# A second kv buffer for a long convolution that runs beside attention, with its load cut into four parts

## The chip, the cores and the metric

The kernel runs on one core of a Trainium2 chip. Its time is the device time of one execution in microseconds (us). The engines are called TensorE or PE, VectorE (DVE), ScalarE (ACT), GpSimd (POOL) and SyncE (SP), which here only issues DMAs.

## What is computed

Two independent computations share one kernel, and their results stand side by side in the output. A is a gated convolution over S = 2048 positions and D = 640 channels: a convolution of 4 taps over k, a product with v, a convolution of length 2048 for each channel, and a product with q. B is plain attention with 32 heads of 20 channels.

```python
def A(q, k, v, shift_k, ssm_k, ssm_D):            # [1, 2048, 640]
    k_pad = pad(k, ks - 1 rows in front)           # ks = 4
    k_shift = sum(k_pad[:, t:t+S] * shift_k[:, ks-1-t] for t in range(ks))
    kv = k_shift * v
    y  = causal_convolution(kv, ssm_k)             # 2048 taps for each channel, by FFT in the reference
    return q * (y + kv * ssm_D)

def B(x, wqkv, wo):                                # H = 32, Dh = 20
    q, k, v = split(x @ wqkv)
    p = softmax(q @ k.T * Dh ** -0.5)
    return (p @ v) @ wo

out = concatenate([A, B], axis=-1)                 # [1, 2048, 1280]
```

## The kernel before

**Attention.** The 32 heads form 8 groups of four; the 2048 queries form 4 blocks of 512, the keys 16 blocks of 128. A tile of scores is 128 keys by 512 queries of one head, and there are 8 x 4 x 16 x 4 = 2048 of them. PE makes the scores (`S_task`, L629), two or three tiles to neighbouring banks of PSUM. ScalarE takes the exponentials of these two or three in one instruction (L671) and writes them to one of 44 slots in SBUF. Some tiles go to VectorE instead: L691 scales a tile out of PSUM, and lines L726 to L731 with L721 or L723 finish the exponential for two tiles together with a polynomial. `want_vec` opens such a chain only when VectorE has little work waiting. PE multiplies the exponentials with v (L749).

**Convolution.** First the short convolution (`C_task`, PE L559, VectorE L580) makes kv, which is written to a scratch tensor in DRAM, `kvr_scratch`. The long convolution is then 40 tasks of 16 channels each (`conv_task`), in 8 blocks of five. Its matmuls (L1022, 128 in a task) take their weights from `HK`, four buffers that are filled from `kext_scratch` (`hk_load`, 16 DMAs in a task), and their moving data from `KVX`, two small buffers in turn. `KVX` for one task is copied by GpSimd out of the kv tile `KVr` in two instructions (`kvx_build`, L994). The kv tile of a block has 80 channels, and so serves five tasks. It is one buffer of 64 x 80 elements in each partition, loaded by `kvr_load` as four DMAs for four sets of 32 partitions, of 320, 240, 160 and 80 KB; what the parts leave open is cleared once by four GpSimd memsets (L972). The call that builds `KVX` for a block's fifth task also asks for the load of the next block, which has to wait until that task's copies have read the tile.

`kvx_build(t + 2)` is called at the end of task t, so a block's last build and the next block's load come at the end of its third task, and the next block's first build comes at the end of its fourth.

**Order.** The whole program is written out by a planner when the kernel is built. It keeps a model clock for each engine, appends to each engine's list whatever is ready by that model, and writes waits for semaphores from its records of who reads and writes which buffer (`Buf`, `Prog.op`). On the chip each engine runs its list in order. PE's loop puts the scores first and fits the rest, convolution included, into the slack that ScalarE leaves. The convolution is paced (`conv_wants`): task n starts when a proportional share of the score tiles has been issued, so that the last starts 230 tiles before the end at the latest. GpSimd's clears and copies wait in a list (`pool_work`), of which one of the first four is placed beside a suitable step of VectorE (`pool_beside`). DMAs on SP are kept in a list too (`P.late`) and appended by `flush` in the order in which the planner finds them ready, with a model of their landing. All DMAs of the trace show the helper's line L239.

**Memory.** The tiles of the short convolution and those of the long one share the region `R`, whose size is the larger of two sums, `ph0` and `ph1`; `conv_setup`, which runs after the last `C_task`, makes the records for the second use.

## Time and profile before

| | |
|---|---|
| three runs | 827.39, 829.12 and 830.6 us; median 829.12 |
| the profiled execution | 825.78 us, its span on the core 824.0 us |
| mean granted TensorE clock | 0.998 |
| convolution matmuls L1022 | 5120, from 168.6 to 766.7 us |
| copies L994 | 80, from 164.6 to 732.2 us, 0.64 us each |
| clears L972 | 4, 0.57 us each, from 144.8 to 149.8 us |
| kext loads | 640 of 136 KB, 3.8 us to landing (median) |
| kvr loads | 32 in 8 groups of four, first group issued at 149.8 us |

In the lines of the profile, "R" stands for everything in the shared region and for the slots of the exponentials, "PS" for PSUM, "issue" for time in which an engine waited for nothing that the profile shows. A group's line has its count, busy time in us and mean in ns of one, then the idle time ahead of it with what ended it. A timeline's line begins with the start and the length in us; instructions of one line that follow each other closely are merged, with the idle time ahead of them in brackets.

### The profile page before, as it was taken

What the parts mean: (1) busy time and instruction counts of PE and PEld (TensorE: products, weight loads), DVE (VectorE), ACT (ScalarE), POOL (GpSimd) and SP (SyncE); (2) the same over time, 40 slices, a digit from 0 to 9 for tenths busy, and PEclk for the clock granted to TensorE, in tenths of its full rate; (3) what the DMA queues carried; (4) which work ended last, traced back from release to release, by engine and by line L of the source; (5) the groups of instructions that cost most, each with busy time, mean ns of one, the idle gap of its engine ahead of it and who ended that gap; (6) DMA issues with size and microseconds to landing.
All of it is one profiled execution on the core that took longest, in us unless ns stands there. A gap on an engine that the chain in (4) does not pass through costs nothing.

```text
span 824.0 us, 27547 instructions
## 1 busy us (share of the span) xinstructions
PE 802.6 (97%) x11750; PEld 368.8 (45%) x11750; DVE 772.6 (94%) x1609; ACT 804.6 (98%) x762; POOL 94.4 (11%) x163
## 2 busy tenths in 40 slices
PE   8999999999999999999999999999999999999997
PEld 4444442244455454444445445544444444453422
DVE  2399999999899999999999999999999999999996
ACT  5999999999899999999999999999999999999996
POOL 3000000111001002210101121000111201010110
PEclk9999999999999999999999999999999999999999
DMA  9934243659878989885898877656887968384111
GB/s 169 313 79 90 44 85 48 137 112 196 171 179 172 197 170 202 180 192 113 167 212 186 171 180 169 151 120 136 181 187 162 192 148 182 98 182 127 28 50 41
DMA packets 163226, 121.94 MB, mean 148 GB/s; under 512 B 72832, under 2 KB 161408, under 8 KB 162848
## 3 DMA queue, kind: packets, MB, share of 16 engines
q1 hardware_dynamic: 160912, 117.06, 66.4%
q0 software_dynamic: 736, 2.75, 0.9%
q8 instruction: 93, 1.52, 0.8%
q10 hardware_dynamic: 1456, 0.37, 0.2%
q14 instruction: 29, 0.24, 0.1%
HBM read 106.83 MB, written 10.61 MB: 143 GB/s over the span
## 4 chain that ended last, share of the span: by engine, by line
ACT 54%; PE 22%; DVE 22%; issue 1%; DMA 1%
ACT R L671 54%; PE PS L629 7%; DVE XV L691 6%; PE PS L1022 6%; PE PS L749 3%; PE PS L484 3%; DVE XF L728 2%; DVE XF L731 2%; DVE XF L726 1%; DVE R L721 1%; DVE XF L727 1%; DVE XF L729 1%; PE PS L846 1%; PE PS L530 1%; DVE R L723 1%; DVE R L1041 1%
## 5 line engine op out<-in xcount | busy, mean ns | idle before, releaser
L671 ACT ACTIVATE R<-PS 128x1024 bf16<-128x1024 f32 (+1 forms) x754 | 800.3, 1265 | 4.4 <-PE PS L629 4.0
L629 PE MATMUL PS<-QT,KT 20*128 20x512 bf16 x2048 | 293.9, 385 | 11.1 <-ACT R L671 5.1
L691 DVE TENSOR_SCALAR XV<-PS 128x512 uint16<-128x512 f32 x291 | 197.7, 684 | 9.1 <-PE PS L629 7.5
L1022 PEld LDWEIGHTS PS<-R 128*128 128x128 bf16 x5120 | 163.3, 97 | 81.3 <-issue 80.8
L1022 PE MATMUL PS<-R 128*128 128x32 bf16 (+5 forms) x5120 | 197.7, 184 | 1.6 <-issue 1.5
L749 PE MATMUL PS<-R,V_sb 128*21 128x512 bf16 x2048 | 160.8, 385 | 0.7 <-DVE R L721 0.2
L629 PEld LDWEIGHTS PS<-QT,KT 20*128 20x128 bf16 x2048 | 73.5, 91 | 195.5 <-ACT R L671 155.0
L731 DVE TENSOR_TENSOR XF<-XF 128x1024 bf16<-128x1024 bf16 (+1 forms) x151 | 100.3, 666 | 0.4
L728 DVE TENSOR_TENSOR XF<-XF 128x1024 bf16<-128x1024 bf16 (+1 forms) x151 | 100.3, 666 | 0.1
L994 POOL COPY R<-R 128x256 uint32<-128x256 uint32 x80 | 51.0, 638 | 392.9 <-DVE XV L691 98.8
L721 DVE TENSOR_TENSOR R<-XF,XV 128x1024 uint16<-128x1024 bf16 x93 | 63.6, 684 | 0.1
L749 PEld LDWEIGHTS PS<-R,V_sb 128*21 128x21 bf16 x2048 | 35.3, 89 | 61.8 <-issue 36.4
L390 PE MATMUL PS<-Zt 128*128 128x512 bf16 x206 | 60.9, 392 | 1.2 <-DVE Zt L384 1.0
L729 DVE TENSOR_SCALAR XF<-XF 128x1024 bf16<-128x1024 uint16 (+1 forms) x151 | 61.6, 410 | 0.1
L727 DVE TENSOR_SCALAR XF<-XF 128x1024 bf16<-128x1024 uint16 (+1 forms) x151 | 61.3, 410 | 0.3
L726 DVE TENSOR_SCALAR XF<-XV 128x1024 uint16<-128x1024 uint16 (+1 forms) x151 | 60.7, 410 | 0.1
L1061 POOL TENSOR_TENSOR R<-R 128x160 bf16<-128x160 bf16 x64 | 31.3, 488 | 182.2 <-DVE XF L726 51.2
L484 PE MATMUL PS<-xT,WQ 128*20 128x512 bf16 (+1 forms) x660 | 48.4, 375 | 1.4 <-DVE XV L691 0.8
L484 PE MATMUL PS<-xT,WKV 128*20 128x512 bf16 (+1 forms) x660 | 48.7, 376 | 0.5 <-DVE XV L691 0.2
L723 DVE TENSOR_TENSOR R<-XF,XV 128x512 uint16<-128x512 bf16 x105 | 40.5, 419 | 0.2
L530 PE MATMUL PS<-WKV,xT 128*128 128x160 bf16 x320 | 35.8, 235 | 0.5
L473 DVE CAST QT<-PS 128x512 bf16<-128x512 f32 (+1 forms) x33 | 22.0, 668 | 9.2 <-PE PS L484 9.0
(58 smaller groups left out, 352.3 us busy)
## 6 DMA issues: line engine op xcount, KB each, us to landing
R<-kext_scratch SPq DMA_DIRECT2D x640, 136.0 KB, 3.8
R<-in_A_v_dram SPq DMA_DIRECT2D x4, 640.0 KB, 5.0
kext_scratch<-in_A_ssm_k_dram POOLq DMA_DIRECT2D x1, 2560.0 KB, 13.4
kvr_scratch<-R SPq DMA_DIRECT2D x128, 20.0 KB
R<-kvr_scratch SPq DMA_DIRECT2D x8, 320.0 KB, 5.1
R<-in_A_q_dram SPq DMA_DIRECT2D x32, 80.0 KB, 3.7
out_dram<-R SPq DMA_DIRECT2D x32, 80.0 KB, 3.3
R<-kvr_scratch SPq DMA_DIRECT2D x8, 240.0 KB, 5.4
```

What stands on the lines that cost most here:

```text
L484: ins = e.matmul(bank[bk][32 * i:32 * i + DH, 0:n], Wt[:, cc, off + i * DH:off + (i + 1) * DH], xT[:, cc, x0:x0 + n], start=(cc == 0), sto ...
L629: ins = e.matmul(bank[b0 + i], KT[32 * u:32 * u + DH, g % 2, kb * 128:(kb + 1) * 128], QT[32 * u:32 * u + DH, qs(qc, g), :], start=True, s ...
L671: P.op("act", lambda e: e.activation(P_sb[:, s0:s0 + m, :], PS[:, b0 * 512:(b0 + m) * 512].rearrange("p (u q) -> p u q", u=m), ACT.Exp, sc ...
L691: work(0.2, [(lambda e: e.tensor_scalar(V, bank[bk], scale * 1.4426950408889634 * 128.0, 127.0 * 128.0, op0=ALU.mult, op1=ALU.add), [bkb[b ...
L721: last = [(lambda e: e.tensor_tensor(o, Q2, V2, ALU.add), bv + [bq], [b_P[z] for z in zs], two, True)]
L726: (lambda e: e.tensor_scalar(F.bitcast(U16), V, 127, None, op0=ALU.bitwise_and), bv, [bf], one, True),
L727: (lambda e: e.tensor_scalar(Q, F.bitcast(U16), -128.0, None, op0=ALU.add), [bf], [bq], one, True),
L728: (lambda e: e.tensor_tensor(Q, Q, F.bitcast(U16), ALU.mult), [bf, bq], [bq], two, True),
L729: (lambda e: e.tensor_scalar(F, F.bitcast(U16), a / 16384.0, b / 128.0, op0=ALU.mult, op1=ALU.add), [bf], [bf], one, True),
L731: (lambda e: e.tensor_tensor(Q, Q, F, ALU.mult), [bf, bq], [bq], two, True)] + last, end)
L749: ins = e.matmul(bank[OBANK][32 * u:32 * u + DH + 1, :], V_sb[:, kb, (4 * g + u) % 16, :], P_sb[:, slot[4 * b + u], :], start=first, stop= ...
L1022: P.op("pe", lambda e, o=o, lhsT=lhsT, rhs=rhs, st=st, k=k: e.matmul(o, lhsT, rhs, start=st, stop=k == 7, skip_group_check=True), reads=rd ...
```

## The change

There are two kv tiles in place of one, used by blocks in turn. Each of the four parts of a tile has its own record and its own semaphore. The load of the next block is asked for in four pieces: the call that builds `KVX` for a block's first task asks for part 0 of the next block, the one for the second task for part 1, and so on; the fifth asks for nothing. The second tile is cleared by four more memsets, which stand in GpSimd's list between the first four and the first copies. The region `R` grows by 5120 elements (10,240 bytes) in each partition.

```diff
-        ph1 = NHK * HK_E + KVR_E + 2 * KVX_E + 128 + 2 * Y_E + NAQ * AST_E
+        ph1 = NHK * HK_E + 2 * KVR_E + 2 * KVX_E + 128 + 2 * Y_E + NAQ * AST_E
...
-        KVr2 = carve(KVR_E)
+        KVr2 = [carve(KVR_E) for _ in range(2)]
         HK = [carve(HK_E) for _ in range(NHK)]
-        KVr = KVr2.rearrange("p (j c) -> p j c", j=64)
-        KVr2 = KVr2.bitcast(U32)
+        KVr = [x.rearrange("p (j c) -> p j c", j=64) for x in KVr2]
+        KVr2 = [x.bitcast(U32) for x in KVr2]
...
-        d_kvr, d_kext, d_small = DS("kvr"), DS("kext"), DS("small")
+        d_kvr, d_kext, d_small = [DS("kvr%d" % a) for a in range(4)], DS("kext"), DS("small")
...
-            cv["KVr"] = Buf(*allx, *b_kvst)
+            cv["KVr"] = [[Buf(*allx, *b_kvst) for _ in range(4)] for _ in range(2)]
...
-            for i in range(4):
-                pool_work(lambda e, i=i: e.memset(KVr2[:, 480 * i:480 * i + 480], 0), [], [cv["KVr"]], 0.55)
-            kvr_load(0)
+            for x in range(2):
+                for i in range(4):
+                    pool_work(lambda e, i=i, x=x: e.memset(KVr2[x][:, 480 * i:480 * i + 480], 0), [], cv["KVr"][x], 0.55)
+                if not x:
+                    kvr_load(0, range(4))
...
-        def kvr_load(b):
-            P.dmas("sp", [(KVr[32 * a:32 * a + 32, 16 * a:64, :].rearrange("p j c -> p (j c)"),
-                           ap(kvr_d, [[5120, 32], [1, (64 - 16 * a) * 80]], 163840 * b)) for a in range(4)],
-                   d_kvr, reads=b_kvd, writes=[cv["KVr"]])
+        def kvr_load(b, parts):
+            for a in parts:
+                P.dma("sp", KVr[b % 2][32 * a:32 * a + 32, 16 * a:64, :].rearrange("p j c -> p (j c)"),
+                      ap(kvr_d, [[5120, 32], [1, (64 - 16 * a) * 80]], 163840 * b), d_kvr[a], reads=b_kvd, writes=[cv["KVr"][b % 2][a]])
...
-                src = sub(KVr2, [[1, 4], [40, 4], [160, 16]], t % 5 * 8 + 4 * h)
-                pool_work(lambda e, dst=dst, src=src: e.tensor_copy(dst, src), [cv["KVr"]], [cv["KVX"][i][h]], PKX)
-            if t % 5 == 4 and t < 39:
-                kvr_load(t // 5 + 1)
+                src = sub(KVr2[t // 5 % 2], [[1, 4], [40, 4], [160, 16]], t % 5 * 8 + 4 * h)
+                pool_work(lambda e, dst=dst, src=src: e.tensor_copy(dst, src), cv["KVr"][t // 5 % 2], [cv["KVX"][i][h]], PKX)
+            if t % 5 < 4 and t < 35:
+                kvr_load(t // 5 + 1, [t % 5])
```

## The prediction

> **What bounds the kernel now.** I read the page first: shares of engines, then the groups.

> ```profile
> span 824.0 us, 27547 instructions
> PE 802.6 (97%) x11750; PEld 368.8 (45%) x11750; DVE 772.6 (94%) x1609; ACT 804.6 (98%) x762; POOL 94.4 (11%) x163
> L671 ACT ACTIVATE R<-PS 128x1024 bf16<-128x1024 f32 (+1 forms) x754 | 800.3, 1265 | 4.4 <-PE PS L629 4.0
> L691 DVE TENSOR_SCALAR XV<-PS 128x512 uint16<-128x512 f32 x291 | 197.7, 684 | 9.1 <-PE PS L629 7.5
> L994 POOL COPY R<-R 128x256 uint32<-128x256 uint32 x80 | 51.0, 638 | 392.9 <-DVE XV L691 98.8
> ```

> The exponentials on ScalarE (L671) fill 800.3 of 824.0 us, and in all that time ScalarE idled 4.4 us ahead of them. So the time is set by how many exponentials ScalarE gets, plus start and tail. The rest of the tiles go to VectorE (L691, 291 of them). GpSimd, whose copies (L994) read the kv tile, is 11% busy.

> Next the same group with its shapes kept apart, which prices one tile:

> ```profile
> L671 ACT ACTIVATE R<-PS 128x1024 bf16<-128x1024 f32 x505 | 494.6, 1121 | 4.1 <-PE PS L629 3.8
> L671 ACT ACTIVATE R<-PS 128x1536 bf16<-128x1536 f32 x249 | 361.8, 1558 | 0.3 <-PE PS L629 0.2
> ```

> 494.6/505 = 0.979 us for two tiles, 361.8/249 = 1.453 us for three. One more tile on ScalarE costs 0.474 us.

> Then the place that the change touches. The kv loads on the page's DMA list (KB each, us to landing), the timeline of ScalarE and PE around the first reload, and of GpSimd behind it:

> ```profile
> R<-kvr_scratch SPq DMA_DIRECT2D x8, 320.0 KB, 5.1
> R<-kvr_scratch SPq DMA_DIRECT2D x8, 80.0 KB, 6.4
> ...
> 205.35 1.82 SPq L239 DMA_DIRECT2D R<-kvr_scratch  x4
> 208.89 8.55 SPq L239 DMA_DIRECT2D R<-kext_scratch  x16
> ...
> 212.21 0.77 PE L1022 MATMUL PS<-R 128*128 128x32 bf16 x21
> 214.43 0.29 PE L1022 MATMUL PS<-R 128*128 128x56 bf16 x5 [1.45 <-issue]
> ...
> 215.09 1.02 ACT L671 ACTIVATE R<-PS 128x1024 bf16<-128x1024 f32 x1 [0.71 <-PE PS L629]
> 216.72 1.02 ACT L671 ACTIVATE R<-PS 128x1024 bf16<-128x1024 f32 x1 [0.61 <-PE PS L629]
> 218.23 1.02 ACT L671 ACTIVATE R<-PS 128x1024 bf16<-128x1024 f32 x1 [0.48 <-PE PS L629]
> 219.86 1.94 ACT L671 ACTIVATE R<-PS 128x1024 bf16<-128x1024 f32 x2 [0.60 <-PE PS L629]
> ...
> 217.79 0.62 POOL L994 COPY R<-R 128x256 uint32<-128x256 uint32 x1 [14.18 <-DVE XV L691]
> 219.99 0.63 POOL L994 COPY R<-R 128x256 uint32<-128x256 uint32 x1 [1.58 <-DVE XF L726]
> ...
> 238.30 0.19 PE L1022 MATMUL PS<-R 128*128 128x32 bf16 x1
> ```

> Read it as one story. The four parts are issued at 205.35 to 207.17 and the last lands at 213.70. The copies of task 5 that read them start only at 217.79, released by VectorE and not by the load, and end at 220.6. Task 5 itself (counting 128 matmuls of L1022 to a task) starts at 238.30. So the load has 4.1 us to spare before its copy and the copy 17.7 us before its task. For the other six reloads the same count gives, from end of copies to start of task: 14.3, 17.8, 14.9, 11.9, 15.4 and 19.5 us. None of the seven reloads is waited for by a task.

> One thing is lost there: PE stood 1.45 us at 212.98 and ScalarE idled 0.71+0.61+0.48+0.60 = 2.4 us, more than half of its 4.4. Before that gap task 3 had issued 5+33+32+26+21 = 117 of its matmuls, so it lies inside the last quarter, where the code waits for no semaphore; the trace names no releaser ("issue").

> [...] SP waited for L994 only 4 times, 1.9 us in all. [...] the 16 kext loads issued from 208.89 took 5.57 us to land on the mean, against a median of 3.8. [...] The trace shows the copies' price: of L731, the 12 that overlapped GpSimd work reading SBUF averaged 0.708 us, the 128 others 0.682.

> **The change part by part.**

> Two buffers. The reload no longer waits for the fifth task's copies. What goes: SP's waits for L994, 1.9 us, with nothing late behind them. Nothing on PE goes, by the slacks above: 0.

> Four more clears. The four of before took 2.3 us (573 ns each) at 144.78 to 149.82, then GpSimd stood idle for 14.74 us until the first copy at 164.56. The new four, 4 x 0.573 = 2.3 us, are placed beside VectorE steps in that gap, while the first load is under way. Hidden: 0. If the cover is gone, the first convolution task (168.6) starts 2.3 us later, which its pace up to the last one at 759.6 absorbs. [...] I take 0.

> DMAs. Still 32 with the same bytes; issue 0.32 to 0.43 us each on SP, before and after. The parts are each on a semaphore of their own, so the first copy of a block waits for four instead of one: three waits more for 8 blocks, on an engine with 392.9 us of idle time ahead of these copies. 0. A part's own wait is for the last copies of the block before, done about a task earlier (a task comes every 15 us). Behind it on SP stand the kext loads and whoever needs them on PE. Bounds: as before, 1.9 us of SP waits, or none. Both are free on ScalarE.

> Burst spread. 800 KB at once become 320, 240, 160 and 80 KB, one in each of four tasks. What can go is the lengthened landing of the kext loads and, if the PE gap at 212.98 came of that crowding, ScalarE's 2.4 us. It coincides with the most crowded stretch, but the other six reloads show no such gap, and the wait has no named cause. Bounds: gain 0 to 2.4 us. I take the middle, 1.2.

> Order. The planner knows when loads land, so from the clears at 145 us onwards it writes another order of all engines. That has no row. Its effect is bounded by the units that VectorE takes. The stage view of L691 counts, from 150 us in steps of 150 us, 60, 58, 57 and 57 tiles: steady to 3 in 60. Three tiles in each of two stretches are 6 x 0.474 = 2.8 us either way. I take 0 and keep ±2.8 for the range.

> Sum against the profiled execution (825.78 us: span 824.0 and 1.8 around it): -1.2, 824.6. That execution stands 3.3 us below the median of the three runs, 829.12. Carried to it: 829.12 - 1.2 = 827.9.

> **The rivals.** Effects within 0.5% (4.1 us) are about what a measurement of this kernel can tell from no change.

> *Faster.* The stall goes (2.4) and the new order gives VectorE 60 tiles in every stretch, 8 more, 3.8 us: 829.1 - 6.2 = 822.9. For: such a stretch exists. Against: VectorE is busy 148.1 to 148.6 of 150 us in the later three, and 8 tiles at 684 ns for L691 alone need 5.5 us, more than its 4.9 us of idle time there, before the polynomial is counted.

> *Slower: VectorE gets fewer tiles.* A chain is opened only when VectorE's backlog is small and three score banks and slots come free together. If the new order puts convolution, evacuations and copies against those moments, tiles fall back to ScalarE at 0.474 us each. It decides from 4.1/0.474 = 9 tiles; with 12 of the 252 that follow 150 us, it is +5.7: 834.8. For: VectorE has no spare time to catch up, and ScalarE none either, so nothing hides a worse order. Against: the steady counts above. Other losses of order (a PE gap as at 212.98 in a new place, 2.4 us each) would have to come twice.

> *The change doesn't do what it says.* SP is in order and waits 187.7 us in all for convolution matmuls, so parts might bunch behind kext loads. They'd still come tasks early: 829.1, no change.

> *The reload was on the path after all.* Seven reloads of some 7 us (1.8 issue, 5.4 landing) would be 49 us, 780. The slacks exclude nearly all of it.

> **How the numbers follow.** No change within 0.5%: 0.62 (0.04 of it for the change that bunches), 827.9; its bounds are 829.1 - 2.4 - 2.8 = 823.9 and 829.1 + 2.8 = 831.9, of which the half per cent cuts the lower at 825.0: own range 825.0 to 831.9. Faster: 0.16 (0.02 for the reload on the path). Slower: 0.22. So 0.16, 0.62, 0.22. The range reaches half way into both outer cases, 823.5 to 835.0.

> **What would show it.** Right: L671 again near 800 us with 1757 tiles on ScalarE; L691 within 285 to 297; the kext loads beside reloads landing in about 3.8 us; four more clears in GpSimd's gap before the first copy; PE's "issue" gap gone or elsewhere. Wrong: L691 below 282 (the slower rival), ScalarE's idle time before L671 above 8 us, SP waits for L994 that hold kext loads, or copies of a block's first task released by a DMA.

## The result and the profile after

| | before | after |
|---|---|---|
| median of 20 runs each | 827.85 us | 834.44 us |
| ratio, with its 95% interval | | 1.0058 [1.0039, 1.0076] |
| the profiled execution | 825.78 us, span 824.0 | 834.68 us, span 832.8 |
| its mean granted TensorE clock | 0.998 | 0.979 |

The changed kernel is slower by 0.6%. The medians in this document count every execution, while a ratio leaves out those more than 1.5% above the fastest of their kernel (three of the 20 of before, none of after), and those have a mean clock of 0.982 or less wherever it is on record; over all 20 the means are 830.3 and 833.1 us. The mean clocks in the table, 0.979 against 0.998, are where this study found the difference.

The page of the kernel after, for comparison with the first block of the prediction, and its row of the granted clock, one digit for each fortieth of the span:

```profile
PE 811.0 (97%) x11744; PEld 369.7 (44%) x11752; DVE 770.8 (93%) x1610; ACT 806.2 (97%) x764; POOL 96.1 (12%) x167
PEclk9999999999999999999669999999999999999999
...
L671 ACT ACTIVATE R<-PS 128x1024 bf16<-128x1024 f32 (+1 forms) x756 | 802.0, 1270 | 11.3 <-PE PS L629 10.8
L691 DVE TENSOR_SCALAR XV<-PS 128x512 uint16<-128x512 f32 x290 | 197.1, 684 | 13.2 <-PE PS L629 12.0
```

ScalarE does what it did (802.0 us against 800.3), VectorE takes 290 tiles against 291. The balance of tiles has not moved. What has grown is ScalarE's idle time before its exponentials, from 4.4 to 11.3 us, nearly all of it (10.8) until TensorE's scores are there. And the clock row has a dip that the row of before has not:

```profile
PEclk9999999999999999999999999999999999999999
```

The stage view of the kernel after around the dip (busy us and count by engine, then granted clock, DMA share, GB/s), and under the dots the same stretch of the kernel before:

```profile
399.00:402.00 3.00, 2.23 (x54) 1.72 (x55) 2.96 (x7) 3.00 (x4) 0.63 (x1) 0.98 0.66 183
402.00:433.00 31.00, 31.00 (x360) 12.74 (x361) 21.39 (x44) 22.64 (x21) 2.54 (x4) 0.51 0.63 149
433.00:464.00 31.00, 30.64 (x496) 14.60 (x492) 30.80 (x64) 30.95 (x31) 3.21 (x6) 1.00 0.65 143
...
402.00:433.00 31.00, 30.31 (x507) 14.12 (x504) 30.68 (x68) 31.00 (x30) 3.69 (x6) 1.00 0.95 197
```

In those 31 us TensorE ran at half clock (0.51), was busy without a gap and yet finished 360 matmuls where the kernel before finished 507. ScalarE worked 22.64 us instead of 31.00, so 8.4 us were lost there; the two spans differ by 8.8 us. In the stretches shown beside it ScalarE loses next to nothing (3.00 of 3.00 and 30.95 of 31.00 us). The rest of the account is smaller: around the gap of before at 213 us the kernel after saves 2.4 us (ScalarE is busy 17.00 us between 205 and 222 us, against 14.59), and some 2.8 us (8.8 + 2.4 - 8.4) are lost in small parts elsewhere, which I did not follow up.

What TensorE did just ahead, in the timeline of the kernel after (L1024 is the convolution matmul, L1043 the last step of VectorE that empties its bank):

```profile
397.69 0.61 PE L749 MATMUL PS<-R,V_sb 128*21 128x512 bf16 x8
398.23 0.39 PE L629 MATMUL PS<-QT,KT 20*128 20x512 bf16 x3
399.77 0.18 PE L1024 MATMUL PS<-R 128*128 128x32 bf16 x1 [1.15 <-DVE R L1043]
399.88 0.39 PE L629 MATMUL PS<-QT,KT 20*128 20x512 bf16 x3
...
402.62 0.61 PE L629 MATMUL PS<-QT,KT 20*128 20x512 bf16 x3
```

The first matmul of convolution task 17 needs the bank that task 16 has just filled, and stands 1.15 us until VectorE has emptied it. That instruction is in TensorE's list in front of the next scores, so everything waits. At 401.9 us the clock is halved: the same three scores take 0.61 us instead of 0.39. It stays so until 432.6. I added up the columns of all matmuls at the rate by which the planner prices them (n columns in n/2400 us; three scores, or four matmuls of L749, count once, because together they take 0.39 to 0.40 us in the timelines, as long as one filler L390 of 512 columns, 392 ns on the mean), in stretches of 3.41 us, the length of the shortest whole half-clock stretch in these two traces. Counted back from 401.9, the last before the halving holds 1.25 us of such work by this estimate, the nine ahead of it between 1.95 and 2.43.

With that, the trace of before reads differently too. Apart from its last half microsecond, its clock record has one short half-clock stretch, from 215.9 to 219.3 us, behind the gap at 212.98 that the prediction looked at; the 3.41 us ahead of it hold 1.28 us. The scores show it in the timeline of before:

```profile
214.65 0.39 PE L629 MATMUL PS<-QT,KT 20*128 20x512 bf16 x3
...
216.07 0.61 PE L629 MATMUL PS<-QT,KT 20*128 20x512 bf16 x3
```

A row of digits in which 9 stands for 0.9 and more hides it.

The clock records show a common step. In these two traces each stretch between two changes of the granted clock, half or full, is a whole multiple of 3.413 us: 3.41 and 604.16 us in before (1 and 177), 3.41, 385.71, 30.72 and 399.36 us in after (1, 113, 9 and 117). The half-clock stretches of the other profiled executions, but for the one with fillers withheld and the pieces cut off by a span's end, last 3.4, 6.8, 13.7, 27.3, 30.7 or 47.8 us; with fillers withheld they go up to 112.6 us. The wait need not be long: here half clock followed a gap of 1.15 us, in 3.41 us that held little work besides.

### The profile page after: what moved, and what is told of

The parts are those of the page before. It is cut to its first block, busy times and chain, and to the rows that moved or that the text cites. A ratio compares the mean times of both kernels' runs of the same rounds, so it can differ in the third digit from the quotient of the medians.

```text
span 832.8 us, 27586 instructions
## 1 busy us (share of the span) xinstructions
PE 811.0 (97%) x11744; PEld 369.7 (44%) x11752; DVE 770.8 (93%) x1610; ACT 806.2 (97%) x764; POOL 96.1 (12%) x167
## 4 chain that ended last, share of the span: by engine, by line
ACT 40%; DVE 31%; PE 27%; issue 1%
ACT R L671 40%; PE PS L629 8%; DVE XV L691 8%; PE PS L1024 8%; PE PS L749 4%; PE PS L484 4%; DVE XF L728 3%; DVE XF L731 3%; DVE R L721 2%; DVE XF L726 2%; DVE XF L727 2%; DVE XF L729 2%; PE PS L390 1%; DVE R L723 1%; DVE R L1043 1%; DVE ZS L1041 1%
## 5 line engine op out<-in xcount | busy, mean ns | idle before, releaser
L671 ACT ACTIVATE R<-PS 128x1024 bf16<-128x1024 f32 (+1 forms) x756 | 802.0, 1270 | 11.3 <-PE PS L629 10.8
L629 PE MATMUL PS<-QT,KT 20*128 20x512 bf16 x2048 | 298.1, 390 | 10.6 <-ACT R L671 3.4
L691 DVE TENSOR_SCALAR XV<-PS 128x512 uint16<-128x512 f32 x290 | 197.1, 684 | 13.2 <-PE PS L629 12.0
L1024 PEld LDWEIGHTS PS<-R 128*128 128x128 bf16 x5120 | 163.7, 97 | 77.3 <-issue 76.1
L1024 PE MATMUL PS<-R 128*128 128x32 bf16 (+5 forms) x5120 | 196.2, 184 | 1.3 <-DVE R L1043 1.3
L749 PE MATMUL PS<-R,V_sb 128*21 128x512 bf16 x2048 | 162.8, 390 | 1.4 <-DVE R L721 0.5
L629 PEld LDWEIGHTS PS<-QT,KT 20*128 20x128 bf16 x2048 | 73.6, 91 | 202.6 <-ACT R L671 161.5
L731 DVE TENSOR_TENSOR XF<-XF 128x1024 bf16<-128x1024 bf16 (+1 forms) x150 | 99.9, 666 | 0.4
L390 PE MATMUL PS<-Zt 128*128 128x512 bf16 x208 | 63.2, 402 | 1.9 <-DVE Zt L384 1.0
L749 PEld LDWEIGHTS PS<-R,V_sb 128*21 128x21 bf16 x2048 | 35.6, 90 | 64.0 <-issue 36.7
L726 DVE TENSOR_SCALAR XF<-XV 128x1024 uint16<-128x1024 uint16 (+1 forms) x150 | 61.0, 411 | 0.2
L721 DVE TENSOR_TENSOR R<-XF,XV 128x1024 uint16<-128x1024 bf16 x85 | 58.2, 685 | 0.1
L484 PE MATMUL PS<-xT,WQ 128*20 128x512 bf16 (+1 forms) x660 | 51.1, 389 | 0.8 <-DVE XV L691 0.6
L723 DVE TENSOR_TENSOR R<-XF,XV 128x512 uint16<-128x512 bf16 x120 | 46.6, 418 | 0.2
```

What stands on the lines that cost most here:

```text
L484: ins = e.matmul(bank[bk][32 * i:32 * i + DH, 0:n], Wt[:, cc, off + i * DH:off + (i + 1) * DH], xT[:, cc, x0:x0 + n], start=(cc == 0), sto ...
L629: ins = e.matmul(bank[b0 + i], KT[32 * u:32 * u + DH, g % 2, kb * 128:(kb + 1) * 128], QT[32 * u:32 * u + DH, qs(qc, g), :], start=True, s ...
L671: P.op("act", lambda e: e.activation(P_sb[:, s0:s0 + m, :], PS[:, b0 * 512:(b0 + m) * 512].rearrange("p (u q) -> p u q", u=m), ACT.Exp, sc ...
L691: work(0.2, [(lambda e: e.tensor_scalar(V, bank[bk], scale * 1.4426950408889634 * 128.0, 127.0 * 128.0, op0=ALU.mult, op1=ALU.add), [bkb[b ...
L721: last = [(lambda e: e.tensor_tensor(o, Q2, V2, ALU.add), bv + [bq], [b_P[z] for z in zs], two, True)]
L726: (lambda e: e.tensor_scalar(F.bitcast(U16), V, 127, None, op0=ALU.bitwise_and), bv, [bf], one, True),
```

## The experiments

Two theories. *Clock theory*: the loads cost nothing; the planner, which sees other landing times, writes another order, and this one leaves TensorE little work in the 3.4 us from 398.5 us, behind which the clock is halved for 31 us. *Load theory*: the early split loads, the extra clears or the second tile cost the time themselves. Each run is compared with the kernel before on the same chip. The edits are abridged.

**Early loads, order of before.** The planner is told of one tile and late loads, so it writes the order of before; the real DMAs go out early.

```diff
-            if t % 5 == 4 and t < 39:
-                kvr_load(t // 5 + 1)
+            # planned as before, but nothing is emitted for it;
+            # when the copies of task t are placed:
+            if t % 5 < 4 and t < 35:
+                P.ops["sp"].append(dma of part t % 5 of block t // 5 + 1, tile (t // 5 + 1) % 2)
```

> The order of before on TensorE, VectorE and ScalarE, instruction for instruction, but with the two kv tiles, the eight clears (two at a time) and the four parts of each reload issued one per task, early. Clock theory (the slower time comes from a stretch at half TensorE clock that the new order brings, not from the loads): ratio 1.000 to before within 0.3%, mean clock 0.99 or more, no half-clock stretch near 400 us. Load theory (the early split loads, the clears or the second tile cost the time themselves): ratio near 1.006 to 1.008, with the clock as it may be.

Measured: 824.76 us against 828.38, ratio 0.996 [0.9942, 0.9978], mean clock 1.0 in the profiled run. Not slower, as the load theory wants, and even a little faster than the clock theory said. (Four of its 22 executions have a mean clock of 0.978, so half-clock stretches are rarer here, not gone.) The place of before's gap in its timeline (L1042 is the convolution):

```profile
213.07 0.91 PE L1042 MATMUL PS<-R 128*128 128x32 bf16 x26
213.95 0.39 PE L630 MATMUL PS<-QT,KT 20*128 20x512 bf16 x3
```

The 21 and 5 matmuls that were 1.45 us apart now run in one go, and no half-clock stretch follows. Between 205 and 222 us ScalarE is busy 17.00 us, against 14.59 in before.

**The changed kernel, filled.** Four idle matmuls more, at no cost in the planner's books so that nothing else moves.

```diff
+                        if (bt, u, k) == (16, 3, 0):
+                            P.op("pe", matmul(bank[OBANK], Zt, zrhs, start=False), ..., tok=False, c=0.0)
```

> The changed kernel with four idle matmuls more (zeros into the attention's output bank, 0.2 us each), placed in the last quarter of convolution task 16, just ahead of the place where TensorE stood 1.15 us at 398.6 us; nothing else moved. Clock theory: the half-clock stretch of 31 us from 402 us is gone in most runs, mean clock 0.99 or more, ratio to before 1.000 within 0.4%, although TensorE has more work. Load theory: no gain, ratio 1.006 or above.

Measured: 824.22 us, ratio 0.9958 [0.9943, 0.9973]. Its timeline at the same task, the inserted matmuls at L1023:

```profile
396.16 0.38 PE L1023 MATMUL PS<-Zt 128*128 128x512 bf16 x1
...
398.67 0.18 PE L1028 MATMUL PS<-R 128*128 128x32 bf16 x1 [0.63 <-DVE R L1047]
398.78 0.39 PE L629 MATMUL PS<-QT,KT 20*128 20x512 bf16 x3
...
402.20 0.39 PE L629 MATMUL PS<-QT,KT 20*128 20x512 bf16 x3
```

TensorE arrives later, waits 0.63 us instead of 1.15, and the scores at 402.20 still take 0.39 us: the clock holds, and the mean clock is 0.994 or more in all 19 executions. Wherever one lays 3.41 us over this place they hold about 1.5 us of work or more; in the kernel after it can be as little as 1.2. Some 0.9 us of useless work (four times 0.21) saved 10 us by the medians.

**The same four elsewhere**, in task 12 (the same edit with 12 for 16).

> The control of the filled kernel: the changed kernel with the same four idle matmuls, but in convolution task 12 (about 334 us) instead of task 16. Clock theory: they don't help, the half-clock stretch from about 400 us stays, ratio near 1.006 (1.003 to 1.010). If any four more matmuls did it, 0.996.

Measured: 835.21 us, ratio 1.0073 [1.0038, 1.0108]; the half-clock stretch is there, from 402.1 us, 30.7 us long. The time is that of the changed kernel, so it isn't the number of idle matmuls that counts but their place.

**Late loads, order of after.** The mirror of the first: planned as in the changed kernel, but one tile, loaded whole after the fifth task's copies.

```diff
-            if t % 5 < 4 and t < 35:
-                kvr_load(t // 5 + 1, [t % 5])
+            # planned as in the changed kernel, but nothing is emitted for it;
+            # when the copies of task t are placed:
+            if t % 5 == 4 and t < 39:
+                P.ops["sp"] += dmas of all four parts of block t // 5 + 1, tile 0
```

> The order of the changed kernel on TensorE, VectorE, ScalarE and GpSimd, but the reloads as before: into one tile, all four parts together, after the fifth task's copies. Clock theory: as slow as the changed kernel, ratio to before near 1.006 (1.003 to 1.010), with the half-clock stretch from about 400 us. Load theory: back to the time of before, ratio 1.000 within 0.3%.

Measured: 835.92 us, ratio 1.0097 [1.0063, 1.0131]. Its clock row, and the two longest waits of TensorE for another engine's or a DMA's work outside the attention:

```profile
PEclk9999999999999999999669999999999999999999
...
PE PS L1041 <- DMA R<-kext_scratch: 1.4, 1, 1.4
PE PS L1041 <- DVE R L1060: 1.3, 2, 1.1
```

The dip is where it was, behind the same wait for VectorE (1.14 us at 400.3); the early, split loads were not its cause. A second one, of 3.4 us from 661.6, follows another wait for VectorE:

```profile
661.52 0.98 PE L391 MATMUL PS<-Zt 128*128 128x512 bf16 x2 [0.93 <-DVE R L1060]
```

The longest wait, 1.40 us for a kext load at 214.2 us, was followed by no half-clock stretch. SyncE also waited longer for the copies ahead of a reload than before (12.2 us in all against 1.9), so this run is not the new order alone. Its ratio and the changed kernel's, 1.0097 and 1.0058, have overlapping intervals.

**Idle matmuls withheld** from before, 151 of 206, the order kept.

```diff
+                if cv and not start and not P.ops["pe"][-1][0]:
+                    P.ops["pe"].pop()          # planned, not emitted
```

> Before, in its order, with 151 of its 206 idle matmuls left out from the convolution's start on; nothing of the result depends on them. Clock theory: TensorE has less to do and yet the kernel is slower, by 1% or more, with several half-clock stretches and a mean clock clearly below 0.99. Load theory, by which TensorE's clock decides nothing here: within 0.5% of before.

Measured: 911.13 us, ratio 1.0987 [1.0934, 1.1041]. The clock row of its profiled execution, the slowest of the four (929.91 us, mean clock 0.812; the others have 0.835 to 0.847):

```profile
PEclk9999995677975695555575576959999999999997
```

The size was underrated: without these fillers TensorE is at half clock for more than a third of the span (a mean of 0.812 over 928.1 us makes some 350 us).

**Which part of the change.** Three runs in the order of before, on TensorE, VectorE and ScalarE instruction for instruction. First, the early loads again, but all four parts at the block's first task:

```diff
-            if t % 5 < 4: part t % 5
+            if t % 5 == 0: parts 0 to 3
```

> As the kernel with early loads in the order of before, but the four parts of a reload are issued together at the block's first task, not one per task. If the gain of 0.4% comes from the loads being spread: back to before, ratio 1.000 within 0.2%, with a burst that can still stop TensorE. If it comes from their being early, or from where the burst falls: ratio near 0.996.

Measured: 827.32 us, ratio 1.0002 [0.9966, 1.0037]. Its profile has no gap at 213 us but a half-clock stretch of 13.7 us from 331.1. This points to the spread of the loads, not their being early, as what gains; but its interval overlaps that of the first run (0.9942 to 0.9978), so it is not shown. Nor does the stretch at 331.1 fit the sum of columns: the 3.41 us ahead of it hold 1.77 us, and no wait over 0.2 us stands in them.

Second, the second tile and the clears, loads late:

```diff
+                    e.memset(KVr2[1][:, 480 * i:480 * i + 480], 0)   # beside each clear of tile 0
-                src = sub(KVr2, ...)
+                src = sub(KVr2[t // 5 % 2], ...)
```

> Before, in its order, with the second kv tile in use and the four clears more, but each reload late and in one piece as before. If tile and clears cost nothing: ratio 1.000 within 0.3%, with the TensorE gap at 213 us as before. If they cost or gain: outside that; and if the gain of 0.4% with early loads came from the second tile, 0.996.

Measured: 841.36 us, ratio 1.0095 [1.0063, 1.0128], a miss for both readings. In this kernel the first and the fifth reload stood four kext loads further ahead in SyncE's list. Its TensorE timeline at these two, in an execution of 851.02 us (those in the ratio have mean clocks of 0.972 to 0.994, so their stretches are fewer or shorter):

```profile
214.74 0.78 PE L1045 MATMUL PS<-R 128*128 128x32 bf16 x21 [1.21 <-DMA R<-kext_scratch]
216.50 0.33 PE L1045 MATMUL PS<-R 128*128 128x56 bf16 x5 [0.97 <-issue]
...
439.97 0.19 PE L1045 MATMUL PS<-R 128*128 128x32 bf16 x1 [1.71 <-DMA R<-kext_scratch]
```

Both times the kext loads behind the reload came late. At the first TensorE stood twice and a half-clock stretch of 30.7 us began at 216.5; after the wait at the second, one of 27.3 us began at 441.8. The same once more with SyncE's list kept as well:

> Before with the second kv tile used in turn and eight clears instead of four, and with every engine's order kept, SyncE's too: a cleaner form of the run with tile and clears only, in which the reload had moved ahead of four kext loads on SyncE. If tile and clears cost nothing, and the 0.95% there came from that place on SyncE: ratio 1.000 within 0.3%. If they cost: 1.005 or more.

Measured: 829.01 us against 828.0, ratio 1.0002 [0.9963, 1.0041]. Second tile and clears cost nothing that shows. What is left between the two runs is the place of the reloads in SyncE's list (and a second semaphore for them), so four places there cost 1%, by way of late kext loads. Written out with the second tile and four more planned clears but the old loads (not run), the program has the order of before on every engine but GpSimd; so the new order comes from the loads' planned times.

**Before, filled at 213 us**: four idle matmuls in task 3, in the manner of the second run.

> Before with four idle matmuls more ahead of its own gap at 213 us, nothing else moved. Clock theory: the stretch of half clock at 216 us goes in most runs, ratio 0.996 to 0.999, without any change of the loads. If the clock there is not decided by TensorE's own activity: 1.000 or slightly above.

Measured: 826.83 us, ratio 0.9991 [0.9967, 1.0015]: not told apart from before, and a miss for the clock theory's forecast. The gap (1.44 us, "issue") and the short half-clock stretch behind it, from 218.2, stay in its profile; the 3.41 us ahead of that stretch hold about 1.3 us, no more than in before. The timeline of TensorE in this run (start us, busy us, operation, count, then the idle time before it):

```profile
215.49 0.20 PE L1026 MATMUL PS<-R 128*128 128x32 bf16 x2
217.13 0.34 PE L1026 MATMUL PS<-R 128*128 128x60 bf16 x6 [1.44 <-issue]
```

The gap lies later by the time of the inserted work, but at the same place in TensorE's list: 21 instructions after the scores, which are 21 convolution matmuls in before and in the two runs with tile and clears only, and 18 of them with three of the inserted four here. In all four kernels it stands behind the 5313th instruction that the trace has of TensorE. So it is tied to a place in the list, not to a time or to VectorE's tile.

The DMA packets give a lead, no more. The page lists a queue q8, "instruction", with 93 packets of 16 KB. In before the last of them to land ahead of the gap's end starts at 211.55 us, 11.5 us after the packet ahead of it, and lands at 212.80, 1.6 us before the gap ends. In the changed kernel, which has no gap there, the same packet starts 8.4 us after the one ahead. The trace does not say what a packet holds, and no run tried it, so the cause of the gap stays open.

**Other orders.** The changed kernel with the loads asked for otherwise, and the planner free to write its own order for each:

```diff
-            if t % 5 < 4 and t < 35: kvr_load(t // 5 + 1, [t % 5])
+            if t % 5 == 0 and t < 35: kvr_load(t // 5 + 1, range(4))       # whole, first task
+            if t % 5 > 0 and t < 35: kvr_load(t // 5 + 1, [t % 5 - 1])     # parts, one task later
```

> The changed kernel, but the whole reload is asked for at the block's first task; the planner writes an order of its own for it (215 idle matmuls; 208 in the changed kernel). Clock theory: the time is that of this order's half-clock stretches, anywhere from 0.996 to 1.012, and the clock tells which: the time follows the mean clock on the same line as in the other runs (about 825 us at 0.998, 835 at 0.979). Load theory: bursts again, so the time of before, 1.000 within 0.2%.

Measured: 842.65 us, the median of six runs that lay too far apart for a ratio: 826.8 us at a mean clock of 0.996, four from 842.0 to 842.9 at 0.970, 851.4 at 0.954. Time follows the clock as the clock theory says, but the medians are 1.8% apart, beyond its 1.2%. The profile, of an execution of 841.97 us, has a half-clock stretch of 47.8 us from 550.8, and at its head the pattern of the changed kernel once more:

```profile
550.47 0.18 PE L1024 MATMUL PS<-R 128*128 128x32 bf16 x1 [0.83 <-DVE R L1043]
```

> The changed kernel, but parts 0 to 3 are asked for at the block's second to fifth task instead of its first to fourth; again an order of its own (203 idle matmuls). The loads are as spread and nearly as early as in the changed kernel. Clock theory: its time need not be that of the changed kernel and follows the mean clock. Load theory: the same as the changed kernel, 1.006 within 0.2%.

Measured: 825.13 us, ratio 0.9956 [0.9935, 0.9977], and no half-clock stretch between 17 and 822 us. One task later, the same loads, and the sign of the result turns.

**More fillers planned**: ZTH from 2.2 to 2.5.

> The changed kernel with the planner's threshold for idle matmuls (ZTH) raised from 2.2 to 2.5 us of TensorE work in 3.4 us, which gives 257 of them instead of 208 and another order. Clock theory: fewer or shorter half-clock stretches and a faster kernel than the changed one, ratio to before 0.995 to 1.002, unless the work that is added comes between ScalarE and its scores. Load theory: no gain, 1.006 or above.

Measured: 824.30 us, ratio 0.9962 [0.9948, 0.9975]. One constant brings the changed kernel to the time that the four placed matmuls gave it, though in another order, so order and fillers are not told apart here. The 51 idle matmuls more than in before cost nothing that shows.

Over all 196 executions of the changed kernel and of the eleven experiments other than the one with fillers withheld, time and mean granted clock go together with a correlation of -0.98; a hundredth of the mean clock is worth about 6.5 us.

## Why the prediction was wrong

The time, 834.4 us, lies just inside the range that the prediction reached with its outer cases, but by luck: that end was priced in tiles, which did not move. The forecast was no change, and it got slower. By its steps:

- *Bound.* Right: ScalarE's exponentials, 1758 tiles against 1757, set the time, and what counts is what keeps them waiting.
- *The reload is not on a task's path.* Right. In the changed kernel SyncE waits for no such copy any more, and the kernel is no faster.
- *Four clears: 0.* Right: 1.0002 with tile and clears alone. They lie between 146.7 and 154.1 us, ahead of the first copy at 166.3.
- *DMA waits and semaphores: 0.* Right in the changed kernel; but I called both bounds free on ScalarE, and the two runs with tile and clears only show a place on SyncE that cost 1%.
- *Burst spread: gain 0 to 2.4 us, 1.2 taken.* Right in sign, too small. In the order of before it brought 0.4% (0.2 to 0.6%), 3.3 us. I counted one execution's idle time at one place, and most of the gain comes by the clock: of the executions with a mean clock of 0.997 or more, those of before on that chip average 825.0 us and those with early loads 824.0. That a burst lengthens the landing of the kext loads rested on one place, 5.57 us against a median of 3.8; why they landed late there is not shown.
- *Order: 0, kept to ±2.8 us by the tiles that VectorE takes.* **This is the step that failed.** The tiles did stay (290). The lists of TensorE, VectorE and ScalarE are those of before up to 220 us, not only up to 145 as I wrote; what changes behind that costs through TensorE's clock, for which the prediction had no term. With late loads in the new order the ratio is 1.0097; with the new order, its own loads and four idle matmuls at the right place it is 0.9958. So the loss is the half-clock stretch of 31 us, 8.4 us of ScalarE's time. The two steps together give 0.996 x 1.0097 = 1.0057, which agrees with the measured 1.0058 but proves little with intervals of 0.2 to 0.35% either way.

The slower rival had the sign but not the mechanism: it priced tiles that fall back to ScalarE. Beside it stood a PE gap in a new place, at 2.4 us each, which would have to come twice. Before the dip it came once, with 1.15 us, and cost 8.4 us, for the gap's price is not the gap but the half clock after it: 3.4 us from 215.9 in before, 30.7 us from 401.9 in after. The cause was in reach of the trace of before. The 2.4 us at 213 us were put down to a 1.45 us stop, and the scores' own duration behind it, 0.61 us instead of 0.39, would have told that the clock was down. And the fillers L390, 206 matmuls that compute nothing, are a sign that the planner pays for a full clock; the prediction did not ask what happens to their work when the order changes.

## What to carry to other kernels

Where a lightly loaded TensorE feeds the bound engine, look for the stretch of a new order with the least TensorE work (here 3.4 us with 1.25 us of work, among others with 1.95 or more) and do not price a wait by itself: here a stop of 1.15 us at the wrong place brought 31 us at half clock, and one of 1.40 us elsewhere none. Ask for the granted clock of short stretches, and look at one matmul shape's duration, before believing a row of nines. When a planner rewrites the whole order, test the change in the old order and the old loads in the new order; the effects here were about -0.4% and +1.0%, and the +0.6% of the whole told neither.

## What was not expected of the hardware

The sum of columns is a guide and does not fit every halving. The profiled executions of before, after and all runs but the one with fillers withheld have twelve halvings after the first 25 us. Ten follow 3.41 us with 0.60 to 1.49 us of work. Two follow more: 1.77 us (331.1 us, whole reload early) and 1.72 (680.7 us, tile and clears only), while in before and after other such stretches with 1.7 to 1.8 us of work were followed by full clock.

The same program falls on either side: of the 20 executions of the changed kernel 16 had a mean clock of 0.977 to 0.981 and took 832.5 to 836.0 us, and four had 0.989 to 0.994 and took 827.8 to 829.5. Before falls on the slower side less often: of the 143 executions of it beside the experiments, 44 had a mean clock of 0.981 or less. What decides it from one execution to the next is not shown.
